# One tuned kernel, three moves of work in time: weight conversion between the first steps, a spread-out inversion, later copies

## The chip, the cores and the metric

The kernel runs on one core of one Trainium2 chip. The metric is the device time of one execution in microseconds (us). Runs of one kernel scatter by some 4 us to either side of their median, mostly with the clock that TensorE is granted. Where two versions ran on different chips, the difference of their medians is given with the one "by the ratios", that is, of each version's ratio to the kernel before on its own chip; the second is the safer.

## The reference

A recurrent attention (RWKV-7) on 4 batches of 8 heads, 768 time steps and 40 channels a head, then a feed-forward network (FFN) with a hard-swish.

```python
# attention, for every batch and head; state is 40 x 40
for t in range(768):
    y[t]  = r[t] @ state
    Sa    = state @ a[t]
    state = state * w[t][None, :] - outer(Sa, b[t]) + outer(v[t], k[t])
# bridge: (4, 8, 768, 40) -> x of (3072, 320)
h = x @ w_in                       # 320 x 2048, given as 64-bit floats
g = h * clip(h + 3, 0, 6) / 6
out = g @ w_out                    # 2048 x 320, given as 64-bit floats
```

## The kernel before

The 768 steps are cut into blocks of 64. A *unit* is one pass over 128 rows for 8 heads; four units make a *group*; there are 24 units, called steps 0 to 23 below, in six groups. For each group a small triangular system (32 x 32 blocks) is inverted on VectorE, which gives `tb`, `tt` and `tinv`. Each step then needs some ten small rounds of TensorE with a copy or an addition of another engine between them. FFN matmuls ("pieces") are put between these rounds to keep TensorE busy. The weights come as 64-bit floats and are converted on the chip: 40 pieces, each with five operations on VectorE and two on ScalarE, through four raw buffers.

Names in the traces: `at`, `bt` and `kt` are inputs of a unit that VectorE scales ahead of its step; `F` holds the blocks to be inverted, `tinv` (or `T`) the inverse. In a step `UT`, `RT` and `VT` are transposes that ScalarE copies for TensorE, `scale` is the decay with which VectorE multiplies the state, `ys` and `yg` are the result before and after its last product, and `xt` is the same result in the FFN's layout.

The order of instructions on each engine is the order in which the Python code below emits them. Generators carry each chain of work; `yield` is a place where something else may be put in.

```python
def invert(F, third):                      # one group's inversion; each yield is a "turn"
    ... transpose F into fb (VectorE), cut out x (GpSimd)
    yield
    for i in range(1, L - 1):              # 30 rounds of two small VectorE operations
        ... prod = x * x ;  yield
        ... x += prod    ;  yield
    tb = ... nc.vector.transpose(...)      # 1.9 us
    yield
    tt = ... nc.vector.transpose(...)      # 2.0 us
    for z in range(0, P, BL):
        nc.scalar.activation(out=tinv[z:z + L, :, 0:L], in_=tb[z:z + L], func=AF.Copy)
        nc.gpsimd.tensor_copy(tinv[z + L:z + BL, :, L:BL], tb[z + L:z + BL])
    third.append((F, tb, tt))
    yield

def aside(n, weight=0):                    # n turns of the inversion, with conversion operations
    for _ in range(n):
        if side and next(side[0], side) is side:
            side.popleft()
        for _ in range(weight):
            next(weights, None)

...
# the first group: prepared first, then its steps
aside(3 * L, 1)                            # the inversion to its end, and on with conversions
fetch("R", 0)                              # the first step's r, on SyncE's DMA queue
...
for t in range(LAST + OWN):                # steps 0 to 3
    for i in range(NU):
        if 0 <= t - APART * i < OWN:
            ...
            run(chains[i], weight=3)       # one stage of a step, three conversion operations in it
...
for _ in weights:                          # what is left of the conversions, all at once
    pass

# the end of a step (it also ends steps 4 to 23)
nc.gpsimd.tensor_tensor(out=yg[:], in0=ys..., in1=o["G"][:], op=ALU.mult)
...
for dst, src in moves[:4]:                 # the attention's result into the FFN's layout:
    nc.sync.dma_start(out=dst, in_=src)    # eight small DMAs, on SyncE's queue too
...
for dst, src in moves[4:]:
    nc.sync.dma_start(out=dst, in_=src)
ready[i] = xt                              # the FFN may use this tile from here on

# the later groups, one slot for each unit
for j, stages in enumerate((
        (before, own, ahead), (before, own, ahead, block, own), (block, own, ahead),
        (own, own, ahead), (own, ahead), (own, own, ahead), (own, ahead), (own, ahead))):
    ...                                    # emit the stages, with moment[1] inversion turns each
    pieces(rate)                           # then FFN pieces
...
elif i % NU == NU - 1:                     # the last unit before a new group
    rates = [(3.25, 3)] * 8                # (FFN pieces, inversion turns a stage) for j = 0 to 7
```

## Time and profile before

| | kernel before |
|---|---|
| time, median of the first 3 runs | 905.53 us |
| span of the profiled run, mean clock | 905.5 us, 0.913 |
| TensorE (PE), VectorE (DVE), ScalarE (ACT) busy | 88%, 59%, 32% |
| TensorE starts on the r of step 0 | 108.60 us |
| first FFN matmul | 144.00 us |
| starts of steps 4 and 5 (first of group 2) | 240.6 and 272.8 us |
| start of step 22 | 815.5 us |

The lines themselves stand in the prediction. To read them: part 2 of the page cuts the span into 40 slices and gives the busy share in tenths; a window line gives the window, its length, then for each engine the busy time and the number of instructions, then the granted clock of TensorE, the share of DMA time and GB/s; a wait line gives the engine and line that waited, what released it, then total time, number of waits and the longest. "Start of a step" is the start of its first matmuls with the state (L576 before, L578 after), which makes it possible to lay two traces side by side.

### The profile page before, as it was taken

What the parts mean: (1) busy time and instruction counts of PE and PEld (TensorE: products, weight loads), DVE (VectorE), ACT (ScalarE), POOL (GpSimd) and SP (SyncE); (2) the same over time, 40 slices, a digit from 0 to 9 for tenths busy, and PEclk for the clock granted to TensorE, in tenths of its full rate; (3) what the DMA queues carried; (4) which work ended last, traced back from release to release, by engine and by line L of the source; (5) the groups of instructions that cost most, each with busy time, mean ns of one, the idle gap of its engine ahead of it and who ended that gap; (6) DMA issues with size and microseconds to landing.
All of it is one profiled execution on the core that took longest, in us unless ns stands there. A gap on an engine that the chain in (4) does not pass through costs nothing. (4 is left out here: it accounts for less than half of the span.)

```text
span 905.5 us, 34874 instructions
## 1 busy us (share of the span) xinstructions
PE 795.4 (88%) x15456; PEld 670.0 (74%) x15456; DVE 533.6 (59%) x1141; ACT 292.0 (32%) x670; POOL 147.8 (16%) x318
## 2 busy tenths in 40 slices
PE   3720289897999999999998999999999998999998
PEld 3620178775788887788887888878888886888886
DVE  7799774678854588543687443695354754222211
ACT  1334563222334422423323343222443223232211
POOL 3221001122121220220220222012022201000000
PEclk7655558997999999999999999999999998999999
DMA  6533541441123222222320222220322111011000
GB/s 130 98 89 104 143 104 30 71 76 35 30 39 66 45 50 35 45 40 44 62 50 15 55 41 50 45 55 11 58 52 45 24 20 25 9 22 24 18 17 15
DMA packets 175974, 45.00 MB, mean 50 GB/s; under 512 B 157904, under 2 KB 173264, under 8 KB 175824
## 3 DMA queue, kind: packets, MB, share of 16 engines
q1 hardware_dynamic: 174768, 42.61, 24.0%
q8 instruction: 122, 2.00, 1.0%
q10 hardware_dynamic: 1056, 0.16, 0.1%
q14 instruction: 28, 0.23, 0.1%
HBM read 34.08 MB, written 3.93 MB: 42 GB/s over the span
## 5 line engine op out<-in xcount | busy, mean ns | idle before, releaser
L771 PE MATMUL o<-wout,gt 128*128 128x320 f32 x768 | 238.4, 453 | 0.2 <-issue 0.2
L747 PE MATMUL h<-xt,win 128*128 128x128 f32 x1536 | 194.0, 278 | 0.9 <-DVE gt L758 0.5
L747 PEld LDWEIGHTS h<-xt,win 128*128 128x128 f32 x1536 | 182.9, 192 | 7.8 <-DVE gt L758 0.7
L771 PEld LDWEIGHTS o<-wout,gt 128*128 128x128 f32 x768 | 142.3, 196 | 52.4 <-issue 4.9
L758 DVE SCALAR_TENSOR_TENSOR gt<-gt,h 128x512 f32<-128x512 f32 x96 | 61.3, 680 | 78.4 <-ACT gt L757 78.4
L364 DVE COPY_PREDICATED score<-mask,any 128x256 f32<-128x256 int32 x143 | 54.8, 437 | 71.3 <-PE any L355 71.3
L757 ACT ACTIVATE gt<-h,three 128x512 f32<-128x512 f32 x96 | 60.7, 684 | 84.9 <-PE h L752 84.9
L505 DVE TENSOR_TENSOR prod<-x 128x30 f32<-128x30 f32 (+9 forms) x180 | 64.8, 360 | 12.1 <-POOL x L497 8.2
L511 DVE TENSOR_TENSOR x<-x,prod 128x30 f32<-128x30 f32 (+9 forms) x180 | 63.2, 351 | 4.8 <-DVE prod L505 0.5
L688 POOL TENSOR_TENSOR yg<-ys,gam 128x512 f32<-128x512 f32 x24 | 31.0, 1291 | 173.0 <-DVE ys L685 138.8
L752 PE MATMUL h<-xt,win 64*128 64x128 f32 x768 | 56.6, 288 | 0.0
L562 ACT ACTIVATE RT<-any 128x512 f32<-128x512 f32 x24 | 14.3, 597 | 119.3 <-PE any L337 119.2
L752 PEld LDWEIGHTS h<-xt,win 64*128 64x128 f32 x768 | 47.4, 190 | 6.8 <-issue 3.7
L379 DVE TENSOR_TENSOR_SCAN prods<-wm,start 128x528 f32<-128x528 f32 x24 | 30.5, 1270 | 28.3 <-ACT wm L376 26.6
L656 DVE TENSOR_TENSOR state<-any,state 128x160 f32<-128x160 f32 x48 | 13.3, 318 | 56.9 <-PE any L649 56.9
L533 PE MATMUL any<-tb,F 32*32 32x32 f32 x768 | 17.8, 204 | 27.5 <-DVE parts L249 20.7
L390 DVE RECIPROCAL gam<-prods 128x256 f32<-128x256 f32 x24 | 41.4, 1737 | 0.0
L404 DVE RECIPROCAL rgam<-prods 128x256 f32<-128x256 f32 x24 | 41.3, 1723 | 0.0
L484 ACT ACTIVATE EV<-any 64x160 f32<-64x160 f32 x92 | 24.7, 294 | 47.6 <-PE any L478 47.0
L685 DVE TENSOR_TENSOR ys<-any,ys 128x256 f32<-128x256 f32 x48 | 18.1, 420 | 36.4 <-PE any L678 36.2
L533 PEld LDWEIGHTS any<-tb,F 32*32 32x32 f32 x768 | 16.0, 119 | 28.8 <-issue 27.1
L337 PE MATMUL any<-ident,R 128*128 128x128 f32 x96 | 15.6, 287 | 24.1 <-DMA R<-in_r_dram 24.1
(138 smaller groups left out, 1182.7 us busy)
## 6 DMA issues: line engine op xcount, KB each, us to landing
raw<-in_moe_w_out_dram SPq DMA_DIRECT2D x20, 256.0 KB
B<-in_b_dram SPq DMA_DIRECT2D x48, 80.0 KB
K<-in_k_dram SPq DMA_DIRECT2D x48, 80.0 KB
V<-in_v_dram SPq DMA_DIRECT2D x96, 40.0 KB
R<-in_r_dram SPq DMA_DIRECT2D x96, 40.0 KB
out_dram<-ob SPq DMA_DIRECT2D x48, 80.0 KB
W<-in_w_dram SPq DMA_DIRECT2D x40, 80.0 KB
A<-in_a_dram SPq DMA_DIRECT2D x40, 80.0 KB
```

Source lines behind the costliest of these rows:

```text
L364: nc.vector.copy_predicated(out=x[:, 4 * i:4 * i + 4, :], mask=mask4, data=o[i][:])
L390: nc.vector.reciprocal(gv[:, :, 0:HB], prods[:, :, 0, 1:HB + 1][:, :, ::-1])
L404: nc.vector.reciprocal(rv[:, :, HB:BL], prods[:, :, 1, 1:HB + 1])
L505: nc.vector.tensor_tensor(out=pv, in0=_ap(x[:], (i + 1) * L + i, [[L, n], [0, i]]), in1=_ap(x[:], i * L, [[0, n], [1, i]]), op=ALU.mult,)
L511: nc.vector.tensor_tensor(out=rest, in0=rest, in1=pv, op=ALU.add)
L533: nc.tensor.matmul(out=zp[x][z:z + L, h, :], lhsT=F[z + L:z + BL, n * H + h, L:BL], rhs=tb[z + L:z + BL, n * H + h, :], start=True, stop=True,
L688: nc.gpsimd.tensor_tensor(out=yg[:], in0=ys[:].rearrange("p r q t -> p r (q t)"), in1=o["G"][:], op=ALU.mult)
L747: nc.tensor.matmul(out=hp[c][:, i, :], lhsT=win[:, t, j * P:(j + 1) * P], rhs=xt[:, t, :], start=(t == 0 and i == 0), stop=False)
L752: nc.tensor.matmul(out=hp[c][:, i, :], lhsT=win2[half(c), (j0 + i) * P:(j0 + i + 1) * P], rhs=xt[half(c), 2, :], start=False, stop=(i == N ...
L757: nc.scalar.activation(out=gt[:], in_=hp[c][:], func=AF.Relu, bias=three[:], scale=1.0)
L758: nc.vector.scalar_tensor_tensor(out=gt[:], in0=gt[:], scalar=6.0, in1=hp[c][:], op0=ALU.min, op1=ALU.mult)
L771: nc.tensor.matmul(out=op[:], lhsT=gts[c][:, n, :], rhs=wout[:, c * HJ + r * NQ + n, :], start=((split or r == 0) and c == 0 and n == 0), ...
```

## The change

The intent has three parts. **Part 1**: the first group's steps begin as soon as the first inversion ends; the weights that are not yet converted then go between the steps' stages. **Part 2**: each inversion gets two empty turns at its start and two at its end, and in the first half of a group's last unit two turns a stage instead of three. **Part 3**: the copies of `T` (that is `tinv`) come later by a turn each (these are the same two turns at the end), and the copy of the prepared unit's `F` (with `bt` ahead of it) comes behind its slot's FFN pieces. No instruction's arithmetic changes. The whole diff:

```diff
@@ invert: parts 2 and 3
-        yield
+        for _ in range(3):
+            yield
         for i in range(1, L - 1):
@@
         tt = inv.tile([P, NH, L], F32, name="tt")
         nc.vector.transpose(...)
+        third.append((F, tb, tt))
         for z in range(0, P, BL):
+            yield
             nc.scalar.activation(out=tinv[z:z + L, :, 0:L], in_=tb[z:z + L], func=AF.Copy)
             nc.gpsimd.tensor_copy(tinv[z + L:z + BL, :, L:BL], tb[z + L:z + BL])
-        third.append((F, tb, tt))
         yield
@@ the first group: part 1
-    aside(3 * L, 1)
+    while side:
+        aside(1, 1)
     fetch("R", 0)
@@ slot: part 3
-                (own, own, ahead), (own, ahead), (own, own, ahead), (own, ahead), (own, ahead))):
+                (own, own, ahead), (own, pieces, ahead), (own, own, ahead), (own, ahead),
+                (own, ahead))):
@@
-                if stage is block:
+                if stage is pieces:
+                    pieces(rate)
+                elif stage is block:
@@
-            pieces(rate)
+            if pieces not in stages:
+                pieces(rate)
@@ the last unit before a new group: part 2
-            rates = [(3.25, 3)] * 8
+            rates = [(3.25, 2)] * 4 + [(3.25, 3)] * 4
```

## The prediction

> **What bounds it now.** I started from the page: TensorE is busy 88% of 905.5 us, VectorE 59%, weight loads 74%. Part 2, the forty slices, shows where TensorE is not:
>
> ```profile
> PE   3720289897999999999998999999999998999998
> ...
> DVE  7799774678854588543687443695354754222211
> ...
> PEclk7655558997999999999999999999999998999999
> ```
>
> One slice is 22.6 us. From the seventh slice on TensorE is nearly full; in the first six it is not, its granted clock is 0.5 to 0.7, and VectorE is the full engine. So I cut the span by stages with the view of busy time by window (columns: window, length, PE, weight loads, VectorE, ScalarE, GpSimd, clock, DMA share, GB/s):
>
> ```profile
> 45.00:108.60 63.60, 6.96 (x192) 6.45 (x193) 61.84 (x200) 27.78 (x66) 8.47 (x14) 0.51 0.41 114
> 108.60:144.00 35.40, 32.27 (x781) 28.36 (x781) 24.29 (x76) 19.46 (x45) 2.50 (x5) 0.55 0.35 86
> 144.00:164.00 20.00, 19.53 (x545) 17.80 (x544) 6.53 (x17) 5.58 (x13) 3.53 (x7) 0.98 0.24 44
> ...
> 480.00:658.00 178.00, 172.16 (x3542) 145.30 (x3542) 102.28 (x201) 59.75 (x134) 29.84 (x61) 0.98 0.23 42
> 658.00:835.00 177.00, 172.65 (x3328) 143.86 (x3330) 79.39 (x174) 52.86 (x113) 23.67 (x46) 0.98 0.14 28
> ```
>
> In 45 to 108.6 VectorE works 61.8 of 63.6 us and TensorE 7; in 108.6 to 164 VectorE has 55.4 - 30.8 = 24.6 us free. Work could move from the first stretch into the second. Later, TensorE idles only 5.8 us in 178 and 4.4 us in 177. The waits of TensorE name the gaps (total, times, longest), first for 0 to 150, then for 150 to the end:
>
> ```profile
> PE any L337 <- DMA R<-in_r_dram: 24.1, 1, 24.1
> PE any L533 <- DVE parts L249: 20.7, 1, 20.7
> ```
>
> ```profile
> PE any L533 <- DVE tb L514: 5.9, 2, 4.4
> PE any L355 <- DVE kt L463: 5.3, 2, 3.8
> PE any L428 <- DVE bt L414: 3.9, 4, 1.5
> PE any L355 <- ACT UT L663: 3.6, 3, 1.6
> ```
>
> The second wait, 20.7 us, ends with the first inversion (its last transpose is the real releaser: it starts at 80.57 and L533 at 82.63). The largest, 24 us, is for the r input of the first step. Why does that input come so late? The timeline of the DMA-issuing queue (start, length):
>
> ```profile
> 85.39 1.91 SPq L228 DMA_DIRECT2D raw<-in_moe_w_out_dram  x2
> 88.46 15.73 SPq L228 DMA_DIRECT2D raw<-in_moe_w_in_dram  x24
> 104.29 0.39 SPq L228 DMA_DIRECT2D raw<-in_moe_w_out_dram  x1
> 104.72 2.58 SPq L320 DMA_DIRECT2D R<-in_r_dram  x4
> ```
>
> The request for r stands behind 12 more weight loads; each waits until VectorE has freed a raw buffer by converting a piece. From 84.4 to 106 VectorE does nothing but convert, one piece each 1.53 us. So the "DMA" wait is a VectorE stretch with nothing of TensorE's in it.
>
> **What the Trainium skill says.** "TensorE: Matmul & The Clock Gate", the table at the top, calls VectorE's and ScalarE's queues strict FIFO: what is put ahead of a step's small operation delays it. The trace agrees: the state scaling of step 0 starts at 106.11, at its place behind the conversions. The same page, section "What's actually happening", has the array's clock gated to half until about 3.4 us of sustained activity, and again after an idle window. The trace agrees only in part: after the 24 us gap the clock stays at 0.50 from 113 to 125, though TensorE is busy 11.96 of those 12 us; only the dense FFN matmuls from 144 on hold it at 0.98. "SBUF — State Buffer", section "Who interferes with whom", says a VectorE instruction with two SBUF inputs blocks against a GpSimd instruction that reads SBUF. Agreed: an inversion product of 58 columns takes 0.84 us at 210.0, beside GpSimd multiplies, and 0.22 us at 239.5.
>
> **Part 1, weights between the steps.** No instruction's work is added or removed. At present the first steps begin after 27 converted pieces; in the new order the request for r stands behind piece 15. That is 12 pieces x 1.53 us = 18.4 us. From the timelines: piece 27's last operation starts at 104.03 and TensorE starts on r at 108.60, 4.57 us later. Piece 15's comes right after the second transpose of the inversion: the first transpose now at 80.57, some 0.4 us later for two more conversion operations in front, a conversion operation of 0.33 between the transposes, the second ending near 85.0. So r's matmuls should start near 85.0 + 4.5 = 89.5, **19.1 us** earlier, and 4 to 5 us of the 24 us wait remain.
>
> The 12 pieces come back inside the steps, three operations a stage, as now but for longer. From 108.6 to the first FFN matmul at 144 the order of TensorE is unchanged and it is the limit (32.3 of 35.4 busy at half clock), so this stretch shifts whole. After it, 12 pieces x 1.45 us of busy time = 17.4 us fall in the next 20 us, where VectorE has 6.5 us of work: 23.9 us, too much for 20, though some pieces begin earlier. The sequencer that issues DMAs also gets the weight loads between the steps' transfers, at 0.65 us a request. I take **2 us** back for both. The second FFN job is put off until all 40 pieces are converted, but contraction matmuls of the first take its place, so TensorE has the same amount in between. Part 1: 19 - 2 = 17 us.
>
> **Part 2, inversions spread.** Two empty turns at the start and two at the end of each inversion, and two turns a stage instead of three in half a unit. In group 1's steps this puts the first kt ahead of two inversion operations and takes an FFN operation of 1.28 us from before the second: the 3.8 and 1.55 us waits for kt lose about 1.5 us. But the inversion of the second group now ends behind a scan of 1.2 us and two operations of 0.2, and TensorE has one FFN piece (1.06 us) less before it needs the transpose: that wait of 1.6 us grows by about **2.5 us**. In the last group, thirteen small operations remain after the state scaling instead of four, about 4 us, but the FFN operation, for which VectorE now idles 3.15 us, moves behind the transpose: of the 4.4 us perhaps 1 goes. Sum: 0.
>
> **Part 3, T's copies later, F behind the FFN pieces.** The two copies of T (ScalarE, 1.05 us each) now stand right before the copy of UT; that costs TensorE 1.63 + 1.63 + 0.36 us. In the new order UT is ahead of them. FFN matmuls between the step's own stage and the prepared unit's fourth stage give VectorE time for bt: waits of 1.54 and 1.33. Sum 6.5 us, of which I expect three quarters, **5 us**. After such gaps the clock falls (0.83 in 490 to 500: 10 us x 0.17 = 1.7 us); that gap closed, 1.5 us more. TensorE has no other idle time there to win.
>
> Sum: 17 + 0 + 5 + 1.5 = 23.5 us; 905.5 - 23.5 = **882.0 us**.
>
> **Rivals.** (a) VectorE is only moved, not relieved: it worked 90% of 45 to 144, and its strict order makes each small step operation wait up to three conversions (0.9 us). If conversions set the pace up to the fortieth piece, the gain of part 1 falls to about 10 us: 891. Against it: 24.6 us of free VectorE time in that stretch for 18 us of work. (b) TensorE stays at half clock longer, because gaps between the steps grow or the second group's waits pass the cooling point: a stretch such as 218 to 228, now at clock 0.57, costs 4 us each. One more makes 886, one fewer 878. (c) The DMA request queue becomes the wait: 35 weight requests x 0.65 = 23 us, four r fetches of 2.6 and two output moves of 5.2 make 44 us in some 55; a late xt would hold the first FFN matmul by 2 to 4 us: 885. (d) Parts 2 and 3 win nothing, as those waits are refilled by the next late operation: 888.
>
> **Range and chances.** The shift of 17 us rests on a transfer's place in the queue and is firm to about 4; the rest, 6.5 us, to about 5; clock luck adds 4 either way. Together about 8: **874 to 892**. Two per cent of 905.5 is 18.1 us, so the line is 887.4; my middle is 5.4 beyond it. Faster by over 2%: 0.74; within 2%: 0.25; slower: 0.01.
>
> **What would show it.** The wait for r falls from 24.1 to about 5 us and TensorE starts on r near 89.5; the first FFN matmul comes near 125 with the order of TensorE before it unchanged; VectorE is over 85% busy from 89 to 140. The UT and bt waits after 271 go; the tb wait near 220 grows to some 4 us. The prediction is wrong if the first FFN matmul comes after 130, if new waits for VectorE of over 5 us stand between 110 and 150, or if the clock from 150 to 230 is below 0.85.

## The result, and the profile after

The changed kernel took **890.66 us** (median of 4 runs, 889.35 to 893.17) against 905.37 us for the kernel before in the same rounds (4 runs, 904.04 to 906.87). A ratio here is the mean time of one kernel's runs over the mean of the other's runs of the same rounds, so it is not quite the quotient of the medians. It is 0.984, with a 95% interval of 0.9812 to 0.9869: 14.7 us less, which is within 2%. The time lies inside the predicted range of 874 to 892; the middle of 882.0 was 8.7 us too low, and the outcome that had been given 0.74, faster by over 2%, did not come. All outputs are right.

Part 2 of the page of the changed kernel (span 889.8 us, mean clock 0.921; one slice is 22.2 us):

```profile
PE   3721968797899999999999999999999998999998
...
DVE  7899677858955488644597544696455746222211
...
PEclk7655568888999999999999999999999998999999
```

The fifth slice, 89 to 111 us, shows the earlier start: TensorE has gone from 2 tenths to 9. But in the sixth to eighth slices it is at 6, 8 and 7 tenths, and the clock, which before was 0.8, 0.9, 0.9 and 0.7 in the seventh to tenth slices, is 0.8 in all four. Here is the timeline of TensorE around the start of the steps (start, length, what; in brackets the idle time just before and what ended it):

```profile
82.46 1.92 PE L535 MATMUL any<-tb,F 32*32 32x32 f32 x64 [21.80 <-DVE tb L515]
88.17 1.44 PE L337 MATMUL any<-ident,R 128*128 128x128 f32 x4 [3.78 <-DMA R<-in_r_dram]
```

The matmuls on r start at 88.17 instead of 108.60, 20.4 us earlier, after a wait of 3.8 instead of 24.1 us. That is what part 1 was to do. Then the lead melts. The next table, taken from the starts of the steps in the traces, shows how far each kernel is ahead of the kernel before (us; the last three rows are experiments explained below).

| kernel | step 0 | step 3 | step 4 | step 5 | step 12 | step 20 | step 22 |
|---|---|---|---|---|---|---|---|
| changed kernel | 20.2 | 13.2 | 6.7 | 5.2 | 9.2 | 15.2 | 17.6 |
| part 1 alone | 23.1 | 14.0 | 7.3 | 5.8 | 6.7 | 5.7 | 13.5 |
| changed, moves on GpSimd's queue | 20.2 | 15.9 | 17.1 | 12.8 | 17.0 | 23.0 | 25.4 |
| changed, old rates | 20.1 | 14.9 | 11.5 | 9.0 | 17.5 | 24.2 | 31.9 |

By step 5 the changed kernel has 5.2 us left of 20.2; from step 5 to step 22 it gains 12.4 us. So both halves of the prediction's sum were off: it had some 16 us at step 5 and 7.5 us after it.

Where did the 15 us go? VectorE is not the answer: in the window from 89 to 140 us it is busy 36.7 of 51 us, 72%, although many conversions are still to be done. The waits of VectorE between 88 and 160 us, and of ScalarE in the same window:

```profile
DVE parts L244 <- DMA raw<-in_moe_w_out_dram: 4.4, 4, 2.0
DVE parts L244 <- DMA raw<-in_moe_w_in_dram: 4.0, 1, 4.0
```

```profile
ACT parts L246 <- DVE parts L244: 25.4, 16, 5.7
```

L244 is the first operation of a conversion. VectorE stands still for raw weights, once for 4.0 us; before, it had no such wait between 108 and 165 us. ScalarE's conversion operations wait behind VectorE's, once for 5.7 us, and since ScalarE too works in order, that step's copy of UT comes behind one of them: TensorE then waits 4.7 us for UT at 127.0. So why were the weights late? The timeline of SyncE's queue (start, time spent on issuing, line, what, number of requests):

```profile
113.27 1.40 SPq L228 DMA_DIRECT2D raw<-in_moe_w_in_dram  x2
114.76 3.22 SPq L703 DMA_DIRECT2D xt<-yg  x4
118.03 3.43 SPq L707 DMA_DIRECT2D xt<-yg  x4
121.57 1.91 SPq L228 DMA_DIRECT2D raw<-in_moe_w_in_dram  x4
...
126.89 4.51 SPq L228 DMA_DIRECT2D raw<-in_moe_w_out_dram  x4
135.17 3.47 SPq L703 DMA_DIRECT2D xt<-yg  x4
```

Between two weight loads stand the eight moves of a finished step's result. Issuing them takes 3.22 + 3.43 = 6.65 us, some 0.8 us each, and no weight load is requested from 114.67 to 121.57; the one that VectorE waits for (until 125.09) is among those that follow. With the next step's moves it is worse: SyncE stands still from 131.40 to 135.17, since the move in front has to wait for `yg`, and what waits in front holds all behind it. These are two of SyncE's waits between 80 and 175 us:

```profile
SPq L703 <- POOL yg L690: 4.8, 1, 4.8
SPq L703 <- POOL scale L567: 4.0, 1, 4.0
```

The second is the one just told; its releaser is named by the semaphore event nearest in time, and GpSimd's `yg` ends just before that `scale`. The first, of 4.8 us, stands later, from 150.7 to 155.6. The last weight load has been issued by then (at 148.0), so it holds back no weights but the second group's inputs: B and W are requested at 161.9 and 163.4, and TensorE waits 3.0 us for W at 166.7 (2.7 us before). This is rival (c) of the prediction with its main effect the other way round: it is not the moves that come late behind the weights, but the weights, and later the inputs, behind the moves.

The page "DMA: Bandwidth & Descriptors" of the Trainium skill, section "Anatomy of one DMA", says that "any semaphore wait happens on the issuing sequencer before dispatch". The 3.8 us without a request agree.

In the later groups the waits of TensorE after 260 us are (all there are):

```profile
PE any L578 <- DVE state L569: 3.2, 3, 1.4
PE any L535 <- DVE tb L515: 2.8, 1, 2.8
```

The waits for UT and bt, which part 3 aimed at, are gone, and the last group's wait for tb fell from 4.4 to 2.8 us. In their place came a wait for the scaled state at L578, at the first step of a group (steps 8, 12 and 16). It did not exist before.

### The profile page after: what moved, and what is told of

Its sections match the earlier page's. It is cut to its first block, busy times and chain, and to the rows that moved or that the text cites. A ratio compares the mean times of both kernels' runs of the same rounds, so it can differ in the third digit from the quotient of the medians.

```text
span 889.8 us, 34847 instructions
## 1 busy us (share of the span) xinstructions
PE 796.2 (89%) x15456; PEld 674.5 (76%) x15456; DVE 536.6 (60%) x1141; ACT 291.5 (33%) x670; POOL 147.8 (17%) x318
## 4 chain that ended last, share of the span: by engine, by line
PE 69%; DVE 6%; POOL 2%; issue 1%; ACT 0%; POOLq 0%
PE o L773 20%; PE h L749 16%; PE any L337 7%; PE h L754 6%; PE any L355 3%; PE any L651 2%; PE any L680 2%; PE any L428 2%; PE any L535 1%; DVE x L512 1%; PE any L633 1%; PE any L612 1%; DVE prod L506 1%; PE any L547 1%; PE any L578 1%
## 5 line engine op out<-in xcount | busy, mean ns | idle before, releaser
L773 PE MATMUL o<-wout,gt 128*128 128x320 f32 x768 | 232.3, 444 | 1.5 <-DVE gt L760 1.5
L749 PE MATMUL h<-xt,win 128*128 128x128 f32 x1536 | 198.0, 281 | 0.0
L749 PEld LDWEIGHTS h<-xt,win 128*128 128x128 f32 x1536 | 187.7, 196 | 6.0 <-issue 0.2
L773 PEld LDWEIGHTS o<-wout,gt 128*128 128x128 f32 x768 | 138.9, 192 | 51.6 <-DVE gt L760 1.8
L449 POOL MEMSET Kt<- 128x24 f32 x24 | 2.8, 118 | 238.6 <-PE any L680 238.6
L535 PE MATMUL any<-tb,F 32*32 32x32 f32 x768 | 17.6, 205 | 27.7 <-DVE tb L515 27.7
L379 DVE TENSOR_TENSOR_SCAN prods<-wm,start 128x528 f32<-128x528 f32 x24 | 30.4, 1267 | 19.2 <-ACT wm L376 17.5
L246 ACT ACTIVATE parts<-parts,low 128x256 uint32<-128x256 uint32 x40 | 20.4, 509 | 55.5 <-DVE parts L244 55.3
```

Source lines behind the costliest of these rows:

```text
L535: nc.tensor.matmul(out=zp[x][z:z + L, h, :], lhsT=F[z + L:z + BL, n * H + h, L:BL], rhs=tb[z + L:z + BL, n * H + h, :], start=True, stop=True,
L749: nc.tensor.matmul(out=hp[c][:, i, :], lhsT=win[:, t, j * P:(j + 1) * P], rhs=xt[:, t, :], start=(t == 0 and i == 0), stop=False)
L773: nc.tensor.matmul(out=op[:], lhsT=gts[c][:, n, :], rhs=wout[:, c * HJ + r * NQ + n, :], start=((split or r == 0) and c == 0 and n == 0), ...
```

## The experiments

Two theories stood after this reading. **Theory A**: part 1 is worth only the 5 us that step 5 shows, and parts 2 and 3 bring some 10. The rival is the prediction's own split, 17 and 6.5. For the lost part of part 1, **theory Q** has the moves in SyncE's order as the cause, **theory V** the conversions in front of the steps' small operations on VectorE. (In the expectations below, "theory A", "theory B", "theory P" and "the rival" are named anew for each run, and each text says what it means by them.) The first four kernels ran on one chip, five rounds each; the kernel before took 906.55 us there (902.69 to 910.52, 11 runs).

### Part 1 alone

```diff
 (kernel before)
-    aside(3 * L, 1)
+    while side:
+        aside(1, 1)
```

> Part 1 alone on the kernel before. Theory A (part 1's gain is given back inside the first group, by step 4 of the second group only some 6 of the 20 us are left; the rest of the change earned the other 10): 899 to 902 us, 4 to 6 less than before. The rival, the prediction's own split (part 1 brings 17 us, the rest little): 888 us. In the profile: the wait for r about 4 us instead of 24, and VectorE waiting for raw weight loads 6 us or more in total.

Measured: 893.36 us (890.23 to 898.88), ratio 0.9865 (0.983 to 0.9901), so 1.35% or some 12 us. Both expectations missed. The trace tells why: the lead is 5.8 us at step 5 as theory A says, but another 6.3 us come between steps 20 and 21, where the last group's wait for tb of 4.4 us is gone. Part 1 has moved the FFN pieces by a few places, so that VectorE's FFN operation of 1.28 us, which stood ahead of the end of the last inversion in the kernel before (and for which VectorE itself waited 3.15 us), now comes behind it. That gain was not part of anybody's reasoning; it is an effect of alignment, and it comes in every version with part 1 and the old rates.

### Parts 2 and 3 alone

This is the changed kernel with `aside(3 * L, 1)` put back.

> Parts 2 and 3 without part 1. Theory A: 895 us (894 to 897), some 10 less than before. The prediction's split: 898 to 900, some 6 less. In the profile: the r wait of 24 us stays; the waits for UT and bt after 271 us are gone and the clock has no dip near 490 us.

Measured: 907.99 us (902.95 to 911.3), ratio 1.0015 (0.9982 to 1.0049): nothing. Both theories fell. The waits for UT and bt are gone in its trace, but two others grew: for the scaled state (4.9 us in three waits) and for the last tb (7.2 us instead of 4.4). Something in parts 2 and 3 eats what the rest of them wins.

### The moves of the first group on GpSimd's queue

```diff
 (changed kernel)
+        mover = nc.gpsimd if i < NU else nc.sync
         for dst, src in moves[:4]:
-            nc.sync.dma_start(out=dst, in_=src)
+            mover.dma_start(out=dst, in_=src)
@@  and the same for moves[4:]
```

> The changed kernel, with the moves of the first group's outputs (xt from yg) issued by GpSimd's queue in place of SyncE's, so that weight loads don't stand behind them. Theory Q (the moves' wait for yg blocks the weight loads, VectorE waits 8.4 us for them, ScalarE behind it): VectorE's waits for raw loads fall below 2 us, ScalarE's wait for the conversions from 25 to some 10, the first FFN matmul comes near 124 instead of 129, and the whole takes 882 to 886. Rival V (there are simply too many conversions in order ahead of the steps' small operations): 889 to 892, and the raw waits go but the UT wait stays.

Measured: 883.09 us (879.49 to 885.04), ratio 0.9737 (0.9707 to 0.9766). That is 7.6 us less than the changed kernel (9.3 us by the ratios), as theory Q has it. Not all of its signs came: ScalarE's wait behind the conversions fell to 18.4 us, where some 10 were expected, and the first FFN matmul came at 125.9, where 124 was. SyncE's timeline at the same place:

```profile
104.62 12.92 SPq L228 DMA_DIRECT2D raw<-in_moe_w_in_dram  x14
117.89 0.39 SPq L228 DMA_DIRECT2D raw<-in_moe_w_out_dram  x1
```

and GpSimd's, with the moves and the operation behind them:

```profile
114.74 2.55 POOL L704 DMA_DIRECT2D xt<-yg  x4 [0.31 <-POOL yg L690]
117.28 2.01 POOL L708 DMA_DIRECT2D xt<-yg  x4
119.30 0.22 POOL L567 TENSOR_TENSOR scale<-last,dec 128x8 f32<-128x8 f32 x1
```

The weight loads now go on until 118.3 us, with the next r behind them. GpSimd makes `yg` itself, so the moves behind it wait for nothing foreign; they do put off the next step's `scale` by the 4.6 us that they take to issue, and TensorE has 1.8 us of waits for the state up to 260 us, against 0.4 in the changed kernel. VectorE's waits for raw weights between 88 and 160 us are gone and TensorE's for UT fell from 7.4 to 2.1 us. The same edit was worth 4.6 us on part 1 alone and 6.5 us on the version with the old rates (both below; 6.1 and 7.7 by the ratios), so it is not an accident of one alignment. By the table above only 2.7 us of the gain are there at step 3, but 10.4 at step 4: between these steps TensorE's idle time falls from 15.1 to 10.9 us and its busy time from 79.3 to 75.8, at a clock of 0.92 instead of 0.87; 2.8 us go again in the second group's first unit, at 0.86 instead of 0.95. The edit takes two things off SyncE's queue at once, the 6.65 us of issuing and the waits for `yg`; no run tells which of them weighs more.

### FFN pieces ahead of F alone

Only the `slot` hunks of part 3, on the kernel before.

> The one move of FFN pieces between the step's and the prepared unit's stage, alone on the kernel before. It should take away the two bt waits of 1.5 and 1.3 us in the steady part and nothing in the first 240 us: 901 to 904 us. If the T copies and the spread inversions earn nothing, it gives all of the 10 us of the rest: 895.

Measured: 905.62 us (900.51 to 907.89), ratio 0.9985 (0.995 to 1.002). The waits for bt are gone, those for UT and the last tb stay. The median is outside both expectations (901 to 904, or 895). No gain can be told from the scatter; the result is inconclusive on whether a microsecond or two is there.

A further kernel, with eight raw buffers for the weights instead of four, was to tell the wait for a request from the wait for a free buffer. It did not build, for want of SBUF; that question stays open.

### Part 1 with the moves on GpSimd's queue, without parts 2 and 3

The next four ran on another chip, where the kernel before took 907.61 us (904.87 to 909.66, 11 runs).

> Part 1 and the output moves of the first group on GpSimd's queue, without parts 2 and 3. The version with all three parts and those moves took 883.1 us. Theory A (parts 2 and 3 earn nothing, as they did alone): 881 to 885. Theory B (the prediction's part 3, 5 to 6.5 us, is there once the first stretch no longer hides it): 887 to 891. The r wait stays near 3 us, step 3 begins some 16 us earlier than before in either case; the UT and bt waits after 271 are back, and the last group's wait for tb should be short or gone, as in part 1 alone.

Measured: 888.74 us (888.15 to 891.61), ratio 0.9798 (0.9777 to 0.9819). Theory B's range: once the first stretch is relieved, parts 2 and 3 bring 5.5 us by the ratios (0.9798 to 0.9737), in spite of what eats at them.

### Part 2 undone

The version with the moves on GpSimd's queue, with one turn at the inversion's start and the old rates. The two turns at its end, which are part 3's, stay.

```diff
-        for _ in range(3):
-            yield
+        yield
@@
-            rates = [(3.25, 2)] * 4 + [(3.25, 3)] * 4
+            rates = [(3.25, 3)] * 8
```

> All three parts and the moves on GpSimd's queue (883.1 us), with part 2 undone: one empty turn at the start of an inversion and three turns a stage again. Theory A (part 2 costs what part 3 wins: its late transposes give the second group's tb wait of 3.1 us, the last group's of 2.8 us and a colder clock behind each): both waits fall to under 1.7 us, the clock in the 36 us after the second group's first step rises from 0.86 to 0.93 or more, time 876 to 880. Theory B (part 2 is neutral, as predicted): 882 to 885.

Measured: 878.19 us (876.1 to 880.16), ratio 0.9664 (0.9643 to 0.9684): some 5 us faster (6.6 by the ratios) than with part 2, as theory A has it. The last tb wait went and the second group's fell to 1.6 us; the clock behind the second group's first step stayed at 0.85, so that part of the theory was wrong. The next run but one shows that the two edits pull in opposite directions.

This run and that of the section before, both on this chip, differ in part 3 and nothing else, so they show what part 3 is worth beside part 1: 888.74 against 878.19 us, **10.5 us**. In the traces step 0 comes 5.0 us later with part 3, but from step 5 to step 20 it wins 11.2 us: TensorE's idle time there falls from 11.3 to 3.5 us and its busy time by 3.5.

### Two conversion operations a stage instead of three

```diff
-                run(chains[i], weight=3)
+                run(chains[i], weight=2)
```

> All three parts and the moves on GpSimd's queue (883.1 us), with two conversion operations a stage between the first group's steps instead of three. Theory V (conversions ahead of the steps' small operations in VectorE's and ScalarE's order cost the 4 us that are given back between steps 0 and 3): steps 0 to 3 are given back 2 us or less and the waits for UT and U (2.1 and 1.6 us) shrink by half; time 879 to 881 if the pieces that are left over at the end of the steps hide, 883 to 886 if they put off the second FFN job and TensorE idles for it. Rival (half clock and the matmuls themselves set the pace): step 3 no earlier than in the version with three, time 883 or more.

Measured: 919.76 us (916.67 to 923.91), ratio 1.0128 (1.0102 to 1.0153): some 35 us slower than with three by the ratios. In one point theory V is right: from step 0 to step 3 only 1.1 us of the lead is given back instead of 4.3, so the conversions between the small operations do cost some 3 us there. But what is left over is then converted in one go behind the steps, with TensorE waiting (waits of TensorE, 85 to 260 us):

```profile
PE any L337 <- DVE score L364: 19.7, 1, 19.7
```

By step 4 the lead is 2.4 us. Both theories had missed this loop, and with it the size: VectorE's work has to be done somewhere, and two operations a stage are too few to get it done beside TensorE. Numbers other than two and three were not tried.

### Only the rates undone

The version with the moves on GpSimd's queue, keeping the empty turns.

```diff
-            rates = [(3.25, 2)] * 4 + [(3.25, 3)] * 4
+            rates = [(3.25, 3)] * 8
```

> All three parts and the moves on GpSimd's queue (883.1 us), with only the rates of part 2 undone (three inversion turns a stage in all of a group's last unit). At most six inversion operations instead of thirteen are left behind the state scaling of the last group's first step. Theory A: the last group's wait for tb of 2.8 us goes and the clock of that stretch of 55 us rises from 0.94 to 0.98 or more, time 878 to 881, with the second group's wait for tb at 3.1 us as it is. Rival (the FFN operation on VectorE takes the place ahead of the transpose, as in the kernel before): wait of 3 to 5 us, time 883 to 885.

Measured: **872.85 us** (870.59 to 873.61, 4 runs), ratio 0.9609 (0.9588 to 0.9631). It is the fastest version. One line was worth 10.2 us (11.6 by the ratios), more than theory A had said. Against it, undoing the empty turns as well (the run before the last) costs 5 us. The timelines of SyncE show the reason for most of that: with one turn at the start,

```profile
78.05 8.00 SPq L228 DMA_DIRECT2D raw<-in_moe_w_out_dram  x3
86.10 7.32 SPq L320 DMA_DIRECT2D R<-in_r_dram  x8
```

and with three,

```profile
78.17 3.98 SPq L228 DMA_DIRECT2D raw<-in_moe_w_out_dram  x2
82.21 3.22 SPq L320 DMA_DIRECT2D R<-in_r_dram  x4
```

With one turn, the r of step 0 stands behind a third weight load, whose buffer is not free before the inversion's two transposes are through; it is requested at 86.10 instead of 82.21, and step 0 starts 3.3 us later. It is the prediction's mechanism of part 1 again, one place in a queue.

### The changed kernel with only the rates undone

Three steps remained: the same line on the changed kernel itself and on parts 2 and 3 alone, and its mechanism. These ran on a third chip (kernel before 906.26 us, 902.17 to 911.08, 11 runs). The edit is the last one, on the changed kernel.

> The changed kernel with nothing but the rates of part 2 undone: three inversion turns a stage in all of a group's last unit, not two in its first half. On the version with the moves on GpSimd's queue this one line was worth 10.2 us (883.1 to 872.9). Theory A (the slower rate costs some 3 us at each of two group boundaries and 5 us in the last group, wherever the rest stands): 890.7 - 10 = 878 to 883, with the waits of TensorE for the scaled state (1.4 us, at steps 8 and 12) and for the last group's tb (2.8 us) gone. Rival (the 10 us hung on the alignment of that version): 887 or more.

Measured: 879.37 us (877.26 to 880.7), ratio 0.9694 (0.9666 to 0.9721). Theory A: 11.3 us by the medians, 13 by the ratios. Lines of the stretches from step 8 to 12, 12 to 16 and 20 to 22, first of the kernel before, then of the changed kernel, then of this one (columns: window, length, TensorE, weight loads, VectorE, ScalarE, GpSimd, clock, DMA share, GB/s):

```profile
376.21:505.85 129.64, 126.44 (x2578) 106.85 (x2577) 78.01 (x156) 42.66 (x98) 22.95 (x48) 0.99 0.24 44
505.85:636.53 130.68, 128.39 (x2593) 107.70 (x2593) 79.77 (x156) 42.79 (x98) 22.93 (x48) 0.99 0.24 43
...
758.41:815.47 57.06, 52.71 (x1066) 43.44 (x1064) 17.12 (x36) 19.28 (x35) 6.60 (x11) 0.94 0.09 18
```

```profile
368.81:496.62 127.81, 126.43 (x2576) 107.22 (x2577) 79.27 (x156) 42.87 (x98) 22.70 (x48) 0.99 0.24 45
496.62:622.69 126.07, 125.61 (x2584) 106.73 (x2585) 78.57 (x156) 42.88 (x98) 23.06 (x48) 1.00 0.24 45
...
743.17:797.83 54.66, 51.84 (x1073) 43.09 (x1072) 16.42 (x36) 18.03 (x33) 6.59 (x11) 0.94 0.09 19
```

```profile
363.52:488.37 124.85, 124.85 (x2577) 105.76 (x2576) 79.33 (x156) 42.82 (x98) 22.63 (x48) 1.00 0.25 46
488.37:613.92 125.55, 125.55 (x2585) 106.59 (x2584) 78.80 (x156) 42.83 (x98) 22.99 (x48) 1.00 0.24 44
...
734.21:783.54 49.33, 48.78 (x1073) 40.84 (x1072) 14.41 (x30) 18.01 (x33) 6.60 (x11) 1.00 0.10 21
```

Length and busy time of TensorE are equal in the new rows of a full group: not a tenth of a microsecond is idle between steps 8 and 16, and the clock is 1.00. The work is the same (2577 matmuls); it is shorter, 124.85 instead of 126.43 us busy, and none of it ran at a lower clock. The last wait for tb is 0.5 us and VectorE has 30 instead of 36 operations in the stretch from step 20 to 22, since its inversion ends earlier.

### Parts 2 and 3 alone, with the rates undone

> Parts 2 and 3 on the kernel before, without part 1 and with the old rates. With the slower rates it was 908.0, no gain. Theory A (the rates ate what part 3 won): 896 to 900, that is 5.5 us for the waits for UT, bt and the clock behind them, as the prediction had it, and some 3 to 5 us more for the last group; the last wait for tb (7.2 us) at 4.4 us or below. Rival (part 3 wins nothing by itself): 904 or more.

Measured: 896.12 us (895.61 to 905.62; five of six runs are below 899.1), ratio 0.9902 (0.9863 to 0.9942). Theory A: with the old rates parts 2 and 3 win 8.9 us by the ratio; with the slow ones they won nothing. The last wait for tb is 4.9 us here, a little above what was expected.

The traces give the price of the slow rates in three pairs. Take the lead at step 22 less that at step 5, first with the slow rates and then with the old ones: 17.6 - 5.2 = 12.4 and 31.9 - 9.0 = 22.9 us on the changed kernel; 12.6 and 22.8 with the moves on GpSimd's queue; -1.3 and 8.9 without part 1. The slow rates cost **10.5, 10.2 and 10.2 us**. On the changed kernel 5.2 of them stand between steps 5 and 20 and 5.3 between steps 20 and 22, where the wait for tb falls from 2.8 to 0.5 us and the clock rises from 0.94 to 1.00.

### T's copies of GpSimd on ScalarE

The first of these two halves has a mechanism that can be tested by itself. In GpSimd's timeline of the changed kernel ahead of step 8:

```profile
364.39 1.28 POOL L690 TENSOR_TENSOR yg<-ys,gam 128x512 f32<-128x512 f32 x1 [1.82 <-DVE ys L687]
365.73 2.13 POOL L525 COPY tinv<-tb 32x1024 f32<-32x1024 f32 x2
367.93 0.20 POOL L567 TENSOR_TENSOR scale<-last,dec 128x8 f32<-128x8 f32 x1
```

and in TensorE's:

```profile
368.81 0.68 PE L578 MATMUL any<-state,at 40*64 40x40 f32 x32 [1.37 <-DVE state L569]
```

The inversion now ends so late that both copies of tb by GpSimd stand between `yg` and the next step's `scale`. VectorE scales the state after `scale`, TensorE needs the state: 1.37 us of idle time, after which the clock falls to 0.50 for some 3 us. In the fastest version, with the old rates, the two copies begin 9.9 and 2.4 us ahead of `scale`, both before `yg`, and there is no wait. The test leaves the rates slow and gives the copies to ScalarE:

```diff
 (changed kernel with the moves on GpSimd's queue)
-            nc.gpsimd.tensor_copy(tinv[z + L:z + BL, :, L:BL], tb[z + L:z + BL])
+            nc.scalar.activation(out=tinv[z + L:z + BL, :, L:BL], in_=tb[z + L:z + BL],
+                                 func=AF.Copy)
```

> All three parts with the moves on GpSimd's queue (883.1 us) and the slow rates, but T's two copies of GpSimd done by ScalarE as well. Theory P (at each group boundary two copies of 1.06 us in GpSimd's order put off the decay product by 2.1 us, and so the scaled state, and so TensorE by 1.4 us and its clock by 1.7): the waits for the state of 1.4 us at steps 8 and 12 go, some 3 us at each of the two boundaries, the last group's wait for tb of 2.8 us stays: 876 to 879. Rival (the late transposes on VectorE hold the chain whatever does the copies, or ScalarE's two further copies hold UT): 882 or more.

Measured: 880.06 us (879.27 to 881.23), ratio 0.9706 (0.968 to 0.9733), against 0.9737 with the copies on GpSimd: 0.3%, some 3 us, less than theory P's 4 to 7 and the intervals overlap, so the time alone does not settle it. The trace does: `scale` comes right behind `yg`,

```profile
357.76 1.28 POOL L691 TENSOR_TENSOR yg<-ys,gam 128x512 f32<-128x512 f32 x1 [1.81 <-DVE ys L688]
359.00 0.21 POOL L568 TENSOR_TENSOR scale<-last,dec 128x8 f32<-128x8 f32 x1
```

the waits for the state at steps 8 and 12 are gone, and the stretches from step 5 to 8 and 8 to 12 shrank by 1.4 and 2.5 us (101.06 to 99.64 and 127.75 to 125.29 us). The last wait for tb stays at 2.8 us, as expected. Two microseconds were lost again in the second group's first unit (38.6 instead of 36.6 us at a clock of 0.82), which this edit has no clear part in. So the copies on GpSimd account for some 4 us of the slow rates' price; the half in the last group was only seen to come and go with the rates.

### More FFN pieces ahead of the second group

The fastest version, with `pieces(1)` instead of `pieces(0.75)` in the sixteen turns ahead of step 4.

> The fastest version so far (872.9 us) with one FFN piece instead of three quarters of one in each of the sixteen turns ahead of the second group's first step: four pieces more, at some 1.06 us each of TensorE, for a wait for tb of 3.1 us at 226 us. Theory A (the wait is filled, and the clock of the next 35 us rises from 0.90 to 0.97): 868 to 871. Rival (VectorE's FFN operation of 1.28 us comes ahead of the inversion's end, so the wait stays or moves): 872 to 875.

Measured: 876.12 us (874.37 to 877.91), ratio 0.9663 (0.9633 to 0.9694), against 0.9609 without: no gain, rather a loss. The wait for tb is still 3.1 us, the clock behind it still 0.90, and new waits for `at` (3.5 us in three) and the last tb (1.4 us) stand later. The wait stayed and others came, as the rival had it. That VectorE's share of the pieces moved along with them is the likely reason, but it is only argued; and since the two were run on different chips, no more than "no gain" is said here.

## Why the prediction was right or wrong

**Part 1, the earlier start: right.** 19.1 us earlier at 89.5 were predicted, 20.4 us at 88.17 measured; the wait for r is 3.8 us, predicted 4 to 5. (One slip without effect: L533 reads `tb`, which is the first of the inversion's two transposes, not the last.)

**Part 1, the 2 us given back: wrong, and the largest error of the sum.** By step 5 the changed kernel had given back 15 us of its 20.2. The prediction's sentence, "I take **2 us** back for both", put VectorE and the DMA-issuing queue together, and its picture of VectorE "over 85% busy from 89 to 140" was wrong too: it was 72% busy and waited for weights. The runs showed in its place that SyncE's order is a limit: moving eight requests a step to another queue brings 7.6 us. The prediction had counted that queue's requests (44 us in some 55) in rival (c), but asked of them only whether they would make the moves late. (It also counted too much: its 0.65 us a weight request is the pace of a stretch in which requests wait for buffers; the requests themselves have a median of 0.42 and 0.37 us in that trace.) The cost came from the other side: moves that take 6.65 us to issue just when weights are due, and moves that wait for their data and hold up what stands behind them, weight loads in one case (4.0 us), the second group's inputs in the other (4.8 us). Of the rest, 3 us are conversions in front of small operations (1.1 instead of 4.3 us given back with two a stage). The other 4 us or so are mostly lost between steps 3 and 5. There the versions with the moves on GpSimd's queue and three conversions a stage lose 1.8 to 5.7 us, with clocks of 0.87 to 0.94 between steps 3 and 4 and idle times of 9.9 to 15.1 us, and no run settles why. The first FFN matmul came at 129.0 instead of "near 125".

**Rivals (a) and (b).** (a) had conversions set the pace and 10 us left of part 1; the size was about right (12 us for part 1 alone, of which 6 by an alignment in the last group), the reason was not: VectorE had 14 us free in 89 to 140, and the loads it waited for stood behind the moves. (b) held in its mild form: the clock varies the time by some 4 us.

**Part 2, sum 0: wrong; its rates cost 10 us.** The prediction looked at the tb waits and had them about right: the last group's fell to 2.8 us, where 3.4 had been predicted, with exactly the thirteen operations counted behind the state scaling; the second group's rose to 3.1 us (about 4 predicted). It did not ask what else comes later when an inversion ends later. At the first step of a group that is two copies on GpSimd ahead of `scale`. And it compared the last wait only with the kernel before, not with what part 1 would leave of it: with the old rates it is 0.5 us, and its stretch 49.3 instead of 54.7 us long.

**Part 3, 5 + 1.5 us: right in mechanism, too small in size.** The waits for UT and bt after 260 us are gone in every version that has it. Its share is hidden in the changed kernel by the rates. Where the rates are the old ones, it wins more than predicted: parts 2 and 3 alone 8.9 us, and part 3 by itself, beside part 1, 10.5 us in all and 11.2 between steps 5 and 20. Its FFN half alone wins 0.4 us in that stretch (the trace of that run); T's copies were not run alone, so how the rest is shared stays open. In its discussion only ScalarE's copies of T are counted, though, not GpSimd's; that is how the wait for the state was missed.

**The sum.** The prediction had 16 us by step 5 (17 + 1.5 - 2.5) and 7.5 after it (1 + 5 + 1.5); the traces have 5.2 and, up to step 22, 12.4, of which 1.9 are lost again by the end. The parts do not add: part 1 gives 12 us alone, parts 2 and 3 with old rates 9, the two together 27 (ratio 0.9694 against 906.26 us is 27.7). The 6 to 7 us beyond the sum do not come from the last group, where part 1 alone already has its gain (49.3 us from step 20 to 22, as with all parts). They stand between steps 5 and 20: part 1 alone wins nothing there (-0.1 us), parts 2 and 3 alone 8.7, all together 15.2, and TensorE's idle time in that stretch is 9.8 us before, 11.0 with part 1 alone, 3.7 with parts 2 and 3 and 0.0 with all. Why the last of it goes only when all are together was not tested.

**What it makes of the range.** The range held because two errors of opposite sign, 11 us too much before step 5 and 5 us too little after it, met inside it: that the time fell into it was luck. The chance of 0.74 for over 2% was too high: the firm part, the shift of 17 us, was firm only at its start.

## What to carry to other kernels

When work that feeds on DMAs is put between steps that issue DMAs of their own, read the issuing queue as an in-order engine with waits, and ask of each request not only how long it takes but whether its data is ready when its turn comes; one that had to wait for a result was better placed here on the queue of the engine that makes that result. When an operation is put off, list everything that comes behind it on *every* engine, the cheap copies too: here two copies of 1 us on GpSimd, ahead of a product of 0.2 us, were the difference between a TensorE that is idle 1.4 us at a group's start and one that is never idle. And take a change apart into its lines before keeping it whole: without one of its lines this one is 27 us faster than the kernel before instead of 15.

## What the Trainium skill lacked or had wrong

- "DMA: Bandwidth & Descriptors", section "Issuing engines are not separate DMA queues", has it that using several issuing engines "will only save the time on the sequencer it takes to initiate the DMA, which is usually small relative to the DMA itself". In these runs the choice of the issuer was not small for the kernel: the move of eight requests a step for four steps to another engine saved 7.6, 4.6 and 6.5 us in three pairs of versions. That includes more than the initiating: the waits for `yg` left SyncE's queue too. The page does say that a DMA's semaphore wait is done by the issuing sequencer; this section does not add that a request which waits holds those behind it (4.0 and 4.8 us here).
- The same page, "Anatomy of one DMA", lists about 50 ns for the sequencer's dispatch on GpSimd's path and calls the making of descriptors small. Together these occupied GpSimd for more here: four moves took 2.55 and 2.01 us (0.64 and 0.50 us each). On SyncE, which is another path, the same four took 3.22 us (0.8 us each).
- "TensorE: Matmul & The Clock Gate" puts a cold clock behind an idle window of about 3.4 us, and its rule of thumb allows gaps up to some 3 us. In the changed kernel an idle time of 1.37 us ahead of step 8 was followed by a clock of 0.64, 0.50 and 0.50 in the three microseconds from 371 to 374; the same gap of 1.38 us ahead of step 12 left it at 1.00. So a drop can follow a gap of less than half that length, and does not each time. In the versions with no idle time there the clock stays at 1.00 from step 8 to step 12, which speaks for the gap as the cause.
- The same page's 3.4 us of activity to a full clock agree with that stretch: if the low clock is 0.50, the 0.64, 0.50, 0.50 and 0.83 (over 374 to 376) make some 3.4 us of it, an estimate from these four figures. They do not agree with the first steps of the kernel before, where TensorE is busy 11.96 of 12 us at 0.50. A part of that work is transposes (L337 and L595); whether these count as activity, no run here tests.
